# Attention before two gated layers: the value products of two chunks of keys and two heads made as one run of four

## The chip, the cores and the metric

The kernel runs on one core of one Trainium2 chip. The metric is the time of one execution on the device in microseconds (us); the median of several executions is compared. The engines are TensorE (PE, its weight loads PEld), VectorE (DVE), ScalarE (ACT), GpSimd (POOL) and SyncE (SP, which here issues transfers).

## The reference, cut to what matters

Attention over 4 batches of 12 heads with 448 tokens of 64 numbers, then a gated layer on all 1792 tokens, then a layer of 8 experts of which each token takes one:

```python
scores = scale * np.matmul(q_n, k_n.transpose(0, 1, 3, 2))   # q, k after RMS norm
scores = scores - np.max(scores, axis=-1, keepdims=True)
attn = np.exp(scores)
attn = attn / (np.sum(attn, axis=-1, keepdims=True) + 1e-09)
attn_out = np.matmul(attn, v)
...
x = moe(attn_out)      # (sigmoid(x @ w_gate) * (x @ w_val)) @ w_out
return moe2(x)         # one expert of two matrices for each token, chosen by a router
```

## The kernel before

Two heads of one batch are worked on together, 24 such head pairs, one after another. The 448 keys are cut into four chunks of 112 (CP, NCH). For each head pair there are eight score steps r = 0 to 7: chunk r // 2 of head r % 2. A score step (scores, L391 and L392) makes a 112 x 448 tile of keys against queries in PSUM out of two matmuls; the score tiles have two buffers (tag S). ScalarE turns it into exponentials (L394) in a tile of SBUF (tag PT, six buffers). The exponentials aren't normalised yet; for the divisor most of them are added up on GpSimd (L402), and over_sums adds over the keys with a matmul against ones, 64 columns for each head (rb, L434). There each head has one to three addends, by the stage (ADDS); the early head pairs have two of them, and so four matmuls.

The value product is weigh (L417). For a chunk of keys it takes, for each of the two heads, the chunk's 112 x 64 values as stationary and its 112 x 448 exponentials as moving operand, in fp32. Head 0 writes partitions 0 to 63 of the accumulator av, head 1 partitions 64 to 127, so the two matmuls use two halves of the array's columns. The accumulator has one buffer and gathers four chunks; then ScalarE copies it out (L427). The trace shows each fp32 matmul as two records.

Other work on TensorE around it: the row maxima are made ahead of the scores, one head pair earlier (maxima, m, L368), queries and keys are transposed (pq L309, pk L350), and the negated maxima too (pm L375).

attention is a generator of ticks. In each tick it gives up to two maxima, one score, at odd r one value product, and preparations of the next head pair. LAG and WLAG say how many ticks the scores follow the maxima and the value products the scores. The caller takes a step of the gated layer (glu, with its matmuls recorded at L680) between ticks when a batch is ready, and feeds weights. The final order on each engine is set by a scheduler that moves instructions by its own estimates. The helper beside ties matmuls together: each one after the first is given high priority and follows the one ahead of it.

Of the kernel before, what the change touches and what calls it, by code (L numbers as in the profile page):

```python
# [20 lines left out]
B, H, S, D = 4, 12, 448, 64  # L21
CP = 112
NCH = S // CP
# [82 lines left out]
def tile_kernel(ctx, tc, q, k, v, g_q, g_k, w_gate, w_val, w_out, emb, tau, w1, w2, out):  # L106
    nc = tc.nc
# [9 lines left out]
    def psum(tag, bufs, name):  # L117
        return ps.tile([P, 512], F32, tag=tag, name=name, bufs=bufs)
# [98 lines left out]
    def part_of(j):  # L217
        return slice(j * D, (j + 1) * D)
# [4 lines left out]
    def load(g):  # L223

        b, hp = divmod(g, H // 2)
        heads = slice(2 * hp, 2 * hp + 2)
        qk = [a1.tile([CP, 2, NCH, D], F32, tag="qk", name=f"{n}{g}", bufs=NQK) for n in ("qr", "kr")]

        def tokens(t, z=heads):
            return t[b, z].rearrange("h (p c) d -> p h c d", c=NCH)  # L230

        if g == 0:
            for i, t, j in ((0, q, 0), (1, k, 0), (0, q, 1), (1, k, 1)):
                (nc.scalar if i == 0 and j == 1 else nc.sync).dma_start(qk[i][:, j], t[b, 2 * hp + j].rearrange("(p c) d -> p c d", c=NCH))
            gains()
        else:
            nc.sync.dma_start(qk[0], tokens(q))
            nc.sync.dma_start(qk[1], tokens(k))

        def values():  # L240
            v_ = a2.tile([CP, 2, NCH, D], F32, tag="v", name=f"v{g}", bufs=2)
            nc.sync.dma_start(v_, tokens(v))
            return v_

        return qk, values
# [59 lines left out]
    def q_side(g, qn):  # L305

        pq = psum("T", 3, f"pq{g}")
        for c in range(NCH):
            nc.tensor.transpose(pq[:, c * CP:(c + 1) * CP], qn[:, c].rearrange("p h d -> p (h d)"), ident[:CP, :CP])  # L309
        X = []  # L310
        for j in range(2):
            xs = a2.tile([P, S], F32R, tag="X", name=f"X{g}_{j}", bufs=NX)
            a, z = part_of(j), part_of(1 - j)
            nc.scalar.activation(xs[a], pq[a, :S], AF.Copy, scale=gcol[a])  # L314
            nc.vector.scalar_tensor_tensor(out=xs[z], in0=pq[a, :S], scalar=gcol[a], in1=fv(xs[a]),
                                           op0=ALU.mult, op1=ALU.subtract)
            X.append(xs)
        return X
# [8 lines left out]
    def constants():  # L327

        one64 = state["one64"] = a2.tile([CP, D], F32, name="one64", bufs=1)
        nc.gpsimd.memset(one64, 1.0)  # L330
        identr = state["identr"] = a2.tile([CP, CP], F32R, name="identr", bufs=1)
        nc.gpsimd.tensor_copy(identr, ident[:CP, :CP])

        state["nm"] = [a2.tile([CP, NG + D], F32R, name=f"nm{i}", bufs=1) for i in range(2)]
        for t in state["nm"]:
            nc.gpsimd.tensor_copy(t, mhalf[:CP, 0:1].broadcast_to((CP, NG + D)))
        for i in range(4):
            t = a2.tile([P, S], F32R, tag=f"X2{i}", name=f"X2{i}", bufs=1)
            (nc.scalar.copy if i % 2 else nc.vector.tensor_copy)(t[upper], ident[upper, 0:1].broadcast_to((D, S)))
            shifted.append(t)  # L340
        for i in range(NY2):
            t = a2.tile([P, S], F32R, tag=f"Y2{i}", name=f"Y2{i}", bufs=1)
            (nc.scalar.copy if i % 2 else nc.vector.tensor_copy)(t[upper], ident[upper, D + i % 2:D + i % 2 + 1].broadcast_to((D, S)))
            picks.append(t)
# [35 lines left out]
    def again(g, st):  # L380

        for j in range(2):
            copy_on(DUP[stage(g)][j], shifted[(2 * g + j) % 4][lower], fv(st["X"][j][part_of(j)]))
# [20 lines left out]
    def beside(first, *others):  # L404

        got = first()
        with tc.high_priority():
            for fn in others:
                with tc.issue_after(got.ins):
                    got = fn()  # L410

    def weigh(g, kc, st):

        if kc == 0:
            st["av"] = psum("av", 1, f"av{g}")

        beside(*(lambda j=j: nc.tensor.matmul(st["av"][part_of(j), :S], lhsT=st["v"][:, j, kc], rhs=st["PT"][j, kc],  # L417
                                              start=kc == 0, stop=kc == NCH - 1) for j in (1, 0)))
        if kc == NCH - 1:
            b, hp = divmod(g, H // 2)  # L420
            if b < B - 1:
                xf[b, hp] = gp.tile([P, S], F32, tag="xf", name=f"xf{g}", bufs=6)
            else:
                if hp % 3 == 0:
                    xf["last"] = wp.tile([P, 3, S], F32, tag="r64", name=f"xf{g}", bufs=2)
                xf[b, hp] = xf["last"][:, hp % 3]
            nc.scalar.copy(xf[b, hp], st["av"][:, :S])  # L427
# [21 lines left out]
    def attention():  # L449

        np_ = B * H // 2
        raw = {0: load(0)}
        pair = {0: prepare(0, *raw[0])}
        raw[1] = load(1)
        constants()
        Y, X, st = {}, {}, {}
        X[0] = q_side(0, pair[0][0])
        Y[0] = k_side(0, pair[0][1])
        for t in range(NTICK):
            g, u = divmod(t, NG)  # L460
            if g < np_:
                if u == 0:
                    st[g] = dict(X=X.pop(g), Y=Y.pop(g), PT={}, sum={}, more=([], []),
                                 nm=state["nm"][g % 2])
                for i in range(MB):
                    if u % MB == 0:
                        maxima(g, u + i, st[g])
                if u == VAT:
                    st[g]["v"] = pair[g][2]()
                if u == AGAIN:  # L470
                    again(g, st[g])
                if u == NG - 1:
                    shifts(g, st[g])
            yield
            w, r = divmod(t - NG - LAG, NG)
            if 0 <= w < np_:
                scores(w, r, st[w])
            yield
            w, r = divmod(t - NG - LAG - WLAG, NG)
            if 0 <= w < np_ and r % 2:  # L480
                weigh(w, r // 2, st[w])
            for w in range(max(g - 3, 0), min(g + 1, np_)):
                if t == (w + 2) * NG - 1 + LAG + RLAG[stage(w)]:
                    over_sums(w, st[w])
            if g + 1 < np_ and u == PAT:
                pair[g + 1] = prepare(g + 1, *raw.pop(g + 1))
                if g + 2 < np_:
                    raw[g + 2] = load(g + 2)
            if g + 1 < np_ and u == XAT:
                X[g + 1] = q_side(g + 1, pair[g + 1][0])  # L490
            if g + 1 < np_ and u == YAT:
                Y[g + 1] = k_side(g + 1, pair[g + 1][1])
            yield
# [1087 lines left out]
```

## Time and profile before

| | |
|---|---|
| median of 3 runs | 1213.91 us (1213.56 to 1214.43) |
| profiled execution | 1212.88 us, of which its span is 1211.1 us |
| busy TensorE | 1149.8 us (95%) |
| busy weight loads | 939.8 us (78%) |
| busy DVE | 841.4 us (69%) |
| busy ACT | 665.1 us (55%) |
| busy POOL | 557.6 us (46%) |
| granted TensorE clock, mean | 0.987 of 2.4 GHz |

Shares are of the whole span. Attention runs from the start to about 621 us, mixed with the gated layer of the first batches from about 110 us on; the rest of the gated layer and the experts follow. The records of matmuls overlap in time, since a matmul's end is later than the next one's start; what one holds TensorE for is read from start to start.

### The profile page before, as it was taken

Reading aid. Unit: us, or ns where it says so; the run is one execution under the profiler, and the core shown is the slowest. Engines: PE = TensorE matmul, PEld = TensorE weight load, DVE = VectorE, ACT = ScalarE, POOL = GpSimd, SP = SyncE. Lnnn points to the kernel's source line nnn. Section 1 sums busy time; section 2 is a strip of 40 time slices with the busy share of each in tenths; the row PEclk is TensorE's granted clock in tenths of the full one; section 3 lists DMA queues with packets and bytes.
Section 4 is the critical chain, followed back from the end, with each engine's and each line's share of the span. In section 5 each row is a group of like instructions: output and inputs, shape, how many; then the busy total and the mean of one; then the engine's idle time right before and its main releaser. Section 6 shows DMA issues by size and latency. Waiting matters only on the chain. (4 is left out here: it accounts for less than half of the span.)

```text
span 1211.1 us, 18407 instructions
## 1 busy us (share of the span) xinstructions
PE 1149.8 (95%) x6516; PEld 939.8 (78%) x6517; DVE 841.4 (69%) x1415; ACT 665.1 (55%) x1239; POOL 557.6 (46%) x452
## 2 busy tenths in 40 slices
PE   3998899899999999999989999999998999999996
PEld 2444687677777777774578989998997999999996
DVE  6897889789768766766789983297456566555552
ACT  5888677777666555556644332243213555555652
POOL 4887976679667555657654430043314110011001
PEclk9999999899999999999999999999999999999998
DMA  4212666776632222210132222021256575777763
GB/s 120 57 51 86 211 217 215 225 223 214 202 113 88 92 93 88 83 42 23 56 89 66 66 66 66 27 65 53 80 150 188 160 213 164 231 232 217 219 203 101
DMA packets 151106, 156.15 MB, mean 129 GB/s; under 512 B 6947, under 2 KB 135205, under 8 KB 151010
## 3 DMA queue, kind: packets, MB, share of 16 engines
q1 hardware_dynamic: 148034, 143.07, 39.0%
q0 software_dynamic: 2848, 11.74, 2.8%
q8 instruction: 53, 0.87, 0.3%
q14 instruction: 43, 0.35, 0.1%
q10 hardware_dynamic: 128, 0.11, 0.0%
HBM read 129.74 MB, written 25.91 MB: 129 GB/s over the span
## 5 line engine op out<-in xcount | busy, mean ns | idle before, releaser
L585 DVE TENSOR_TENSOR wl<-wr,wh 128x768 fp32r<-128x768 f32 (+1 forms) x194 | 188.5, 972 | 142.1 <-ACT wh L582 123.5
L582 ACT CAST wh<-wr 128x768 fp32r<-128x768 f32 (+1 forms) x212 | 171.7, 810 | 178.8 <-DMA wr<-in_w_dram 50.6
L369 DVE TENSOR_REDUCE nm<-m 112x1 fp32r<-112x448 f32 x192 | 114.2, 615 | 33.2 <-PE m L368 31.3
L394 ACT ACTIVATE pt<-s 112x448 f32<-112x448 f32 x192 | 102.2, 542 | 63.0 <-PE s L392 57.9
L402 POOL TENSOR_TENSOR sum<-pt,sum 112x448 f32<-112x448 f32 x78 | 108.2, 1397 | 27.4 <-ACT pt L394 27.2
L271 POOL TENSOR_TENSOR ms<-ms,mhalf 112x8 f32<-112x8 f32 x46 | 85.6, 1860 | 36.6 <-ACT ms L270 36.4
L417 PE MATMUL av<-pt,v 112*64 112x448 f32 x384 | 97.1, 585 | 0.5 <-ACT pt L394 0.2
L402 POOL TENSOR_TENSOR sum<-pt,pt 112x448 f32<-112x448 f32 x48 | 60.9, 1273 | 62.0 <-ACT pt L394 54.1
L391 PEld LDWEIGHTS s<-X,Y 128*112 128x112 f32 x192 | 34.5, 180 | 68.0 <-issue 57.0
L391 PE MATMUL s<-X,Y 128*112 128x448 f32 x192 | 81.3, 424 | 5.6 <-ACT pt L394 5.4
L368 PE MATMUL m<-Y,X 128*112 128x448 f32 x192 | 71.7, 409 | 10.1 <-ACT X L314 5.8
L1289 POOL DMA_INDIRECT xe<-x2d,iu_all x16 | 18.6, 1162 | 123.4 <-PE pxe L1314 119.9
L392 PE MATMUL s<-X,Y 128*112 128x448 f32 x192 | 72.2, 382 | 3.2 <-ACT X L378 3.2
L368 PEld LDWEIGHTS m<-Y,X 128*112 128x112 f32 x192 | 34.1, 183 | 32.1 <-ACT Y L321 6.4
L1300 POOL DMA_INDIRECT out_dram<-orow,iu_all x16 | 17.2, 1077 | 89.1 <-ACT orow L1421 78.9
L623 DVE SCALAR_TENSOR_TENSOR wr<-r 128x768 int32<-128x768 int32 x36 | 41.1, 1141 | 24.6 <-ACT r L620 20.9
L625 DVE SCALAR_TENSOR_TENSOR wr<-r,wr 128x768 int32<-128x768 int32 x36 | 54.2, 1506 | 0.5
L680 PE MATMUL ph<-xeh,wh 128*128 128x256 f32 (+2 forms) x336 | 50.3, 284 | 0.0
L680 PE MATMUL ph<-xel,wh 128*128 128x256 f32 (+2 forms) x336 | 49.7, 282 | 0.0
L680 PE MATMUL ph<-xeh,wl 128*128 128x256 f32 (+2 forms) x336 | 49.4, 282 | 0.0
L585 POOL TENSOR_TENSOR wl<-wr,wh 128x768 fp32r<-128x768 f32 x18 | 37.0, 2056 | 20.7 <-ACT wh L582 20.7
L709 POOL TENSOR_TENSOR gl<-sg,gh 128x448 fp32r<-128x448 f32 x24 | 33.0, 1374 | 29.4 <-DVE gh L321 22.1
(778 smaller groups left out, 3050.3 us busy)
## 6 DMA issues: line engine op xcount, KB each, us to landing
wr<-in_w_dram SPq DMA_DIRECT2D x112, 384.0 KB, 3.9
wr<-w SPq DMA_DIRECT2D x72, 384.0 KB, 3.0
w<-wr SPq DMA_DIRECT2D x36, 384.0 KB, 2.8
r<-in_w_gate_dram SPq DMA_DIRECT2D x12, 768.0 KB, 5.0
r<-in_w_val_dram SPq DMA_DIRECT2D x12, 768.0 KB, 4.9
r<-in_w_out_dram SPq DMA_DIRECT2D x12, 768.0 KB, 4.6
wr<-in_w_dram SPq DMA_DIRECT2D x24, 256.0 KB, 2.9
v<-in_v_dram SPq DMA_DIRECT2D x24, 224.0 KB, 3.1
```

Source lines behind the costliest of these rows:

```text
L271: nc.gpsimd.tensor_tensor(m, m, mhalf[:CP, :m.shape[1]], ALU.pow)
L368: nc.tensor.matmul(s_[:CP, :S], lhsT=st["X"][j][:, c * CP:(c + 1) * CP], rhs=st["Y"][j][0], start=True, stop=True)
L369: last["max"] = nc.vector.tensor_reduce(st["nm"][:, 2 * c + j:2 * c + j + 1], s_[:CP, :S], axis=AX.X, op=ALU.max, negate=True)
L391: nc.tensor.matmul(s_[:CP, :S], lhsT=yh[:, z], rhs=st["X"][j], start=True, stop=False)
L392: nc.tensor.matmul(s_[:CP, :S], lhsT=yl[:, z], rhs=st["X2"][j], start=False, stop=True)
L394: last["exp"] = nc.scalar.activation(p_, s_[:CP, :S], AF.Exp)
L402: eng.tensor_tensor(st["sum"][j], p_, st["PT"][j, 0] if kc == 1 else st["sum"][j], ALU.add)
L417: beside(*(lambda j=j: nc.tensor.matmul(st["av"][part_of(j), :S], lhsT=st["v"][:, j, kc], rhs=st["PT"][j, kc], start=kc == 0, stop=kc == N ...
L582: nc.scalar.copy(hi, raw)
L585: eng.tensor_tensor(lo, raw, fv(hi), ALU.subtract)
L625: nc.vector.scalar_tensor_tensor(out=m, in0=high, scalar=-0x80000000, in1=m, op0=ALU.bitwise_and, op1=ALU.bitwise_or)
L680: nc.tensor.matmul(pt[:, :cols], lhsT=wts[i][a], rhs=xs[i][z], start=first and k == 1, stop=last and k == 3 * n)
```

## The change

weigh now takes a tuple of chunks instead of one. It is called at r = 3 and r = 7 with two chunks, where it was called at r = 1, 3, 5 and 7 with one. It issues four matmuls tied together: the newer chunk of head 1 and head 0, then the older chunk of head 1 and head 0. So the first of the four is the one that reads the newest exponentials. The flags start and stop sit on the first and the last chunk in that order. The code behind line 417 stands one line lower: L434 is L435 in the changed kernel, L680 is L681.

```diff
@@ -409,14 +409,15 @@
                 with tc.issue_after(got.ins):
                     got = fn()
-    def weigh(g, kc, st):
-
-        if kc == 0:
+    def weigh(g, kcs, st):
+
+        if 0 in kcs:
             st["av"] = psum("av", 1, f"av{g}")
-        beside(*(lambda j=j: nc.tensor.matmul(st["av"][part_of(j), :S], lhsT=st["v"][:, j, kc], rhs=st["PT"][j, kc],
-                                              start=kc == 0, stop=kc == NCH - 1) for j in (1, 0)))
-        if kc == NCH - 1:
+        beside(*(lambda j=j, kc=kc: nc.tensor.matmul(st["av"][part_of(j), :S], lhsT=st["v"][:, j, kc], rhs=st["PT"][j, kc],
+                                                     start=0 in kcs and kc == kcs[-1], stop=NCH - 1 in kcs and kc == kcs[0])
+                 for kc in reversed(kcs) for j in (1, 0)))
+        if NCH - 1 in kcs:
             b, hp = divmod(g, H // 2)
             if b < B - 1:
                 xf[b, hp] = gp.tile([P, S], F32, tag="xf", name=f"xf{g}", bufs=6)
@@ -477,8 +478,8 @@
                 scores(w, r, st[w])
             yield
             w, r = divmod(t - NG - LAG - WLAG, NG)
-            if 0 <= w < np_ and r % 2:
-                weigh(w, r // 2, st[w])
+            if 0 <= w < np_ and r % 4 == 3:
+                weigh(w, (r // 2 - 1, r // 2), st[w])
             for w in range(max(g - 3, 0), min(g + 1, np_)):
                 if t == (w + 2) * NG - 1 + LAG + RLAG[stage(w)]:
                     over_sums(w, st[w])
```

The order on TensorE, in the part of the program with attention alone (the second head pair's steps s_2 to s_7 and the maxima of the next). The tile names are s for scores with their r, av for the accumulator, pt for exponentials with their r. Before:

```order
L417 MATMUL av_460<-pt_3_466,v_294 64x448
L417 MATMUL av_460<-pt_2_456,v_294 64x448
L391 MATMUL s_5_516<-X_1_225,Y_249 112x448
L392 MATMUL s_5_516<-X_146,Y_154 112x448
L391 MATMUL s_6_528<-X_0_222,Y_245 112x448
L392 MATMUL s_6_528<-X_144,Y_152 112x448
L368 MATMUL m_7_485<-Y_360,X_1_311 112x448
L368 MATMUL m_0_522<-Y_501,X_0_441 112x448
L417 MATMUL av_460<-pt_5_519,v_294 64x448
L417 MATMUL av_460<-pt_4_491,v_294 64x448
L391 MATMUL s_7_552<-X_1_225,Y_249 112x448
L392 MATMUL s_7_552<-X_146,Y_154 112x448
```

A value pair stands ahead of s_5 and another one ahead of s_7.

TensorE in the changed kernel, the same place:

```order
L417 MATMUL av_491<-pt_3_463,v_294 64x448
L417 MATMUL av_491<-pt_2_456,v_294 64x448
L417 MATMUL av_491<-pt_1_434,v_294 64x448
L417 MATMUL av_491<-pt_0_419,v_294 64x448
L391 MATMUL s_5_516<-X_1_225,Y_249 112x448
L392 MATMUL s_5_516<-X_146,Y_154 112x448
L368 MATMUL m_7_482<-Y_360,X_1_311 112x448
L391 MATMUL s_6_528<-X_0_222,Y_245 112x448
L392 MATMUL s_6_528<-X_144,Y_152 112x448
L368 MATMUL m_0_522<-Y_501,X_0_441 112x448
L391 MATMUL s_7_550<-X_1_225,Y_249 112x448
L392 MATMUL s_7_550<-X_146,Y_154 112x448
```

The pair on pt_5 and pt_4 that stood between s_6 and s_7 is gone from there, and the pair on pt_1 and pt_0 has joined that on pt_3 and pt_2. Between the second matmul of s_5 and the first of s_7 there are four rows now; before there were four and the value pair.

TensorE near the end of attention, before, from s_6 of a late head pair (px is a matmul of the router):

```order
L391 MATMUL s_6_5839<-X_0_5312,Y_5402 112x448
L392 MATMUL s_6_5839<-X_140,Y_152 112x448
L368 MATMUL m_6_5775<-Y_5599,X_0_5509 112x448
L368 MATMUL m_7_5778<-Y_5603,X_1_5512 112x448
L417 MATMUL av_5730<-pt_5_5800,v_5495 64x448
L417 MATMUL av_5730<-pt_4_5784,v_5495 64x448
L391 MATMUL s_7_5853<-X_1_5315,Y_5406 112x448
L392 MATMUL s_7_5853<-X_142,Y_154 112x448
L391 MATMUL s_0_5859<-X_0_5509,Y_5599 112x448
L375 MATMUL pm_5789<-identr,nm_137 66x112 x4
L994 MATMUL px_0_0_5825<-beside_1250,x_0_5691 112x136 x2
```

One more px follows and then the pair on pt_7, so four rows stand between it and the second matmul of s_7.

TensorE in the changed kernel, the same place:

```order
L391 MATMUL s_6_5839<-X_0_5312,Y_5402 112x448
L392 MATMUL s_6_5839<-X_140,Y_152 112x448
L368 MATMUL m_7_5775<-Y_5603,X_1_5512 112x448
L391 MATMUL s_7_5851<-X_1_5315,Y_5406 112x448
L392 MATMUL s_7_5851<-X_142,Y_154 112x448
L391 MATMUL s_0_5857<-X_0_5509,Y_5599 112x448
L417 MATMUL av_5784<-pt_7_5854,v_5495 64x448
L417 MATMUL av_5784<-pt_6_5842,v_5495 64x448
L417 MATMUL av_5784<-pt_5_5800,v_5495 64x448
L417 MATMUL av_5784<-pt_4_5781,v_5495 64x448
```

Here the value pairs on pt_5 and pt_7 have become one run, and one row stands between the second matmul of s_7 and the run that reads pt_7.

In all, the 96 pairs of before stand as 48 unbroken runs of four. TensorE's last 3372 rows of 5699 are the same in both.

## Rows read from the trace of the kernel before

**Rows 1.** Windows: stretch, length, busy us (count) of PE, PEld, DVE, ACT, POOL, clock, DMA.
```profile
33.00:110.00 77.00, 74.81 (x350) 36.28 (x348) 68.38 (x114) 63.88 (x134) 65.67 (x51) 1.00 0.21 61
110.00:557.00 447.00, 432.18 (x2108) 322.65 (x2106) 341.20 (x481) 297.84 (x539) 299.44 (x214) 0.98 0.46 146
557.00:621.00 64.00, 61.18 (x283) 35.06 (x283) 49.02 (x77) 39.40 (x81) 44.36 (x37) 0.97 0.19 59
621.00:1211.00 590.00, 569.00 (x3743) 538.03 (x3741) 361.10 (x695) 245.68 (x448) 131.88 (x112) 0.99 0.45 134
```

**Rows 2.** Windows of line L417 alone: PE and PEld busy, clock, DMA.
```profile
33.00:110.00 77.00, 23.83 (x96) 4.84 (x96) 1.00 0.21 61
110.00:557.00 447.00, 56.04 (x222) 11.35 (x220) 0.98 0.46 146
557.00:621.00 64.00, 17.13 (x68) 3.55 (x68) 0.97 0.19 59
```

**Rows 3.** Timeline, TensorE: start us, length us, what; around one value pair.
```profile
48.40 0.36 PE L392 MATMUL s<-X,Y 128*112 128x448 f32 x1
48.60 0.37 PE L368 MATMUL m<-Y,X 128*112 128x448 f32 x1
48.90 0.97 PE L417 MATMUL av<-pt,v 112*64 112x448 f32 x4
49.80 0.46 PE L391 MATMUL s<-X,Y 128*112 128x448 f32 x1
50.10 0.36 PE L392 MATMUL s<-X,Y 128*112 128x448 f32 x1
```

**Rows 4.** Timeline, TensorE: the four sum matmuls of a head pair (L434).
```profile
44.57 0.55 PE L309 MATMUL pq<-ident,qn 112*128 112x112 f32 x4
45.05 0.97 PE L434 MATMUL rb<-pt,one 112*64 112x448 f32 x4
45.85 0.92 PE L434 MATMUL rb<-sum,one 112*64 112x448 f32 x4
46.70 0.46 PE L368 MATMUL m<-Y,X 128*112 128x448 f32 x1
47.00 0.36 PE L392 MATMUL s<-X,Y 128*112 128x448 f32 x1
```

**Rows 5.** Timeline, TensorE's weight loads inside that run.
```profile
45.48 0.14 PEld L434 LDWEIGHTS rb<-sum,one 112*64 112x64 f32 x2 [0.23 <-issue]
45.85 0.14 PEld L434 LDWEIGHTS rb<-sum,one 112*64 112x64 f32 x2 [0.23 <-issue]
```

**Rows 6.** TensorE's waits, 110 to 557 us: total us, times, longest.
```profile
PE pg L680 <- ACT sg L703: 3.6, 3, 2.3
PE s L391 <- ACT pt L394: 2.8, 2, 1.5
```

**Rows 7.** Timeline, TensorE: a value pair that waited (in brackets: idle, releaser).
```profile
42.89 0.97 PE L417 MATMUL av<-pt,v 112*64 112x448 f32 x4 [0.19 <-ACT pt L394]
```

**Rows 8.** Timeline, TensorE: a score that waited for an exponential.
```profile
572.07 0.46 PE L391 MATMUL s<-X,Y 128*112 128x448 f32 x1 [1.34 <-ACT pt L394]
```

**Rows 9.** Timeline, TensorE: scores on both sides of a value pair.
```profile
52.40 0.36 PE L392 MATMUL s<-X,Y 128*112 128x448 f32 x1
...
52.80 0.36 PE L392 MATMUL s<-X,Y 128*112 128x448 f32 x1
...
54.51 0.46 PE L391 MATMUL s<-X,Y 128*112 128x448 f32 x1
```

**Rows 10.** Timeline, ACT: the exponentials of the two scores of rows 9.
```profile
52.80 0.55 ACT L394 ACTIVATE pt<-s 112x448 f32<-112x448 f32 x1 [0.45 <-PE s L392]
...
53.92 0.54 ACT L394 ACTIVATE pt<-s 112x448 f32<-112x448 f32 x1
```

**Rows 11.** Windows: a stretch with waits, and the half-clock stretch behind it.
```profile
112.61:115.55 2.94, 1.83 (x8) 1.04 (x9) 1.04 (x2) 2.89 (x5) 1.73 (x2) 1.00 0.12 29
115.55:118.96 3.41, 3.41 (x11) 1.53 (x10) 2.47 (x4) 3.05 (x6) 1.57 (x1) 0.50 0.25 70
```

## The prediction, made before the changed kernel ran

> **What bounds the kernel now.** I read the share of each engine by stretch first, then TensorE's order of time around the edited line, then who made TensorE wait. The span falls into four stretches that matter [rows 1]: 33 to 110 us is attention alone, 110 to 557 us is attention with the matmuls of the gated layer (L680) filling TensorE between its steps, 557 to 621 us is the end of attention with little filler, and from 621 us on there is no value product left. TensorE (PE) is busy 74.81 of 77.00 us, 432.18 of 447.00, 61.18 of 64.00 and 569.00 of 590.00 [rows 1]. So it sets the pace in all four, and time that it no longer needs is time saved, as far as the next engine follows. Next in the first stretch are DVE at 68.38 us (89%), POOL at 65.67 and ACT at 63.88 of 77; in the second DVE has 76% and ACT 67% [rows 1]. The edited line shows 96 records in the first stretch, 222 in the second and 68 in the third [rows 2]. Each fp32 matmul is two records and a pair of heads is four, so these are 24, 55 and 17 pairs, 96 in all (two records straddle edges).
>
> **What the change removes.** A pair of value products uses 64 columns of the array per head. From its start at 48.90 to the next matmul at 49.80 it holds TensorE 0.90 us [rows 3]. It also makes its neighbours longer: the maximum's matmul ahead of it has 0.30 us before the pair starts (48.60 to 48.90), and the score matmul behind it has 0.30 (49.80 to 50.10), where the same kind of matmul inside a row of full-width ones has 0.20 (48.40 to 48.60) [rows 3]. That is 0.10 at each end, so a pair costs 0.90 + 0.20 = 1.10 us and two pairs 2.20.
>
> The trace of before has the very thing that the change makes: where both heads have two addends, the sums of a head pair stand as four matmuls of 64 columns in the same alternating order (rb, L434). That run goes from 45.05 to 46.70, or 1.65 us, with 0.30 for the matmul behind it (46.70 to 47.00) [rows 4]. The end ahead of it is hidden behind transposes there, so I take 0.10 for it too: 1.65 + 0.20 = 1.85. A merge saves 2.20 - 1.85 = 0.35 us by these rows; their last digit is 0.01, and I use 0.34. Of that 0.20 is one set of ends fewer, and 0.15 is that the run's second half follows without the first's tail (1.65 against 1.80). The order of the changed kernel has all 48 runs as four neighbouring rows, so 48 x 0.34 = **16.3 us**: 55 / 2 x 0.34 = 9.4 in the stretch with filler, 41 / 2 x 0.34 = 6.9 (7.0 by the rounded sum) in the two without. The number of matmuls, exponentials, additions and transfers is the same, and beyond 621 us TensorE's last 3372 of 5699 rows stand in the same order, so nothing is counted there but the earlier start.
>
> One rule speaks against it. The run's weight loads last 0.14 us and begin 0.37 us apart, 45.48 and 45.85, while the matmuls before them stream, and the run's second half takes 0.85 [rows 4, 5]: they cost nothing. The Trainium skill, TensorE: Matmul & The Clock Gate, Part 3, says that LDWEIGHTS overlaps with matmuls in flight "only when row_grp differs"; here every load goes to the same rows. By that rule two more loads in a row would lie open in each run; this case's row says they don't, and the row decides.
>
> **What it moves.** (a) *Where filler stands.* Here 17 or more rows lie between the newest score and the run, save at two places (9 and 4), so the run itself waits for nothing. Freed time can still be lost to ACT and DVE, on which TensorE waits there for 3.6 us (sigmoid), 2.8 us (exponentials) [rows 6] and less. Bounds: nothing lost, or all 9.4. Both engines have a quarter or more of this stretch free, so I take a tenth: 0.9 us.
>
> (b) *The exponential ahead of the run.* The run's first matmul reads the newest exponential, and all of TensorE's queue is behind it. With three rows between the score and the run's start before, TensorE waited 0.19 us [rows 7]; each row fewer adds one matmul's 0.20 [rows 3]. In the order there were six places with three rows; now there are four with three, two with two, one with one. At 0.19, 0.39 and 0.59 that is 0.76 + 0.78 + 0.59 = 2.1 against 1.1: 1.0 us more. Bounds: 0 (ACT late before as well) and 1.34 for each of the seven [rows 8], 9.
>
> (c) *The scores crowd together.* This is the main cost. The score tiles have two PSUM buffers, so a score must wait until the exponential two scores back is done. Before, a value pair lay between: the second matmul of s_5 at 52.40 and the first of s_7 at 54.51 are 2.1 us apart [rows 9]. Now a stretch of four scores has none between them. Its gap is four rows of 0.20 and the matmul itself, some 1.0 us. ACT needs 0.40 to start and 0.55 for the exponential when it is free (52.40 to 52.80, end 53.35), and more when a copy is ahead of it: the score at 52.80 (s_6) got its exponential at 53.92, 1.12 later, with the end at 54.46 [rows 9, 10]. So the gap is just enough for a free ACT and too short for a busy one. In the order I count 26 places in the stretches without filler where three or four rows, and no value or sum run, lie between; before, two, of three and of two rows (and four of a single row, where a score's second half was put off; now there is one). What each costs isn't in the trace: from nothing to 1.34 us, TensorE's longest wait for an exponential in these two stretches [rows 8], 0 to 35 us in all. A cost below nothing isn't excluded for one place, since a wait like that of 572 us may vanish in another order, but it is for the sum, as no engine but TensorE gets less to do. I take the row nearest in kind, 0.19 [rows 7], since ACT has 13 us of the first 77 free and catches up during the 1.65 us run: 26 x 0.19 = 4.9 us.
>
> (d) *At nothing:* value tiles and exponentials are held longer. There are six exponential tiles, and a run frees four of them one score after its newest; the exponential after the next is the first that needs one back. If that were late, ACT and then TensorE would wait as in (c). The accumulator is held from the first run to its copy, shorter than before. Transfers keep their count and their queues.
>
> Sum: 16.3 - 0.9 - 1.0 - 4.9 = 9.5 us. The profiled execution took 1212.88 us (its span 1211.1 and 1.8 around it), so 1203.4; the median of the runs is 1.03 above it: **1204.4 us**.
>
> **The rivals.** *All of it is kept* (chance 0.12): the scheduler puts maxima and transposes so that no exponential is late. The full 16.3 gives 1197.6. A half-clock stretch that follows a wait (2.94 us with TensorE busy 1.83, then 3.41 at 0.50, which is 1.2 instead of 2.4 GHz [rows 11]) may vanish too, worth half its length, 1.7: 1196. Against it: 89% of DVE becomes 94% in the first stretch (77 - 12 x 0.34 = 72.9).
>
> *Exponentials take what the runs gave* (0.12): the 26 places at 0.45 each are 11.7, and the sum 2.7: 1211.2, between 1209 and 1216 with its spread. For it: the score at 52.80 was served late in a stretch in which ACT still had pauses.
>
> *Slower* (0.10): the same places, but ACT's backlog doesn't drain in one run. It decides from 14.4 / 26 = 0.55 us each; at 0.8 the places cost 20.8 and the time is 1213.9 + 6.4 = 1220. Waits as long as that also precede half-clock stretches [rows 8, 11], each 1.7 more. Against it: the 1.65 us run leaves ACT three exponentials' time (0.55 each), and over the first stretch ACT has 13.1 us without work [rows 1].
>
> *Weight loads lie open in a run* (0.02): two loads of 0.14 in each run [rows 5] leave 0.06 of 0.34, 2.9 us in all, less 6.8: 1217.8. This is what the skill's rule above would give; the rb rows speak against it.
>
> *The run isn't run as one* (0.01): the chip serves the second pair as a new run; the 1.65 us row excludes it. 1213.9 or more.
>
> **How the numbers follow.** The forecast has 0.63 and, with places at 0 to 0.37 us, 1199 to 1209. The range for 8 in 10 runs from 1197 (about half of the first rival lies under it) to 1213 (the slower cases lie over it). A difference within 0.2%, 1211.5 to 1216.3, is about what a measurement of this kernel can't tell from no change. Faster: 0.63 + 0.12 + half of the second rival, 0.06, is 0.81. Same: 0.06 + 0.01 + 0.03 of the slower one's near end, 0.10. Slower: 0.07 + 0.02, 0.09.
>
> **What would show it.** Each run of four holds TensorE 1.65 us with 0.30 at its ends: if 1.85 or more, the first step is wrong. TensorE's waits of a score for an exponential grow from some 5 us to about 10, nearly all ahead of 110 us and after 557: if they stay, the first rival holds, if they pass 19, the slower one. The line's 97 us of busy time [rows 2] falls to about 48 x 1.65 plus tails, 83. The stretch with filler ends some 8 us nearer to the attention start, and 621 us comes at about 611. Unforeseen would be a change after attention, or many half-clock stretches more.

## The result, and the profile after

The changed kernel takes 1220.15 us in the median of six executions, the kernel before 1213.74 in the median of six: a ratio of 1.0052, with an interval of 1.0037 to 1.0067. It is slower by about 6.4 us. The forecast was 1204.4, with a range that ended at 1213.

The first lines of the page of the changed kernel: the span, and TensorE's busy time with its share.

```profile
span 1217.1 us, 18407 instructions
PE 1141.6 (94%) x6516; PEld 951.4 (78%) x6517; DVE 841.8 (69%) x1415; ACT 663.5 (55%) x1239; POOL 555.0 (46%) x452
```

Before, TensorE was busy 1149.8 of 1211.1 us. So it is busy 8.2 us less, and idle 75.5 instead of 61.3 us: 14.2 us more. The mean granted clock fell from 0.987 to 0.983 of 2.4 GHz in the two profiled executions; over the six executions of the changed kernel it is 0.982. The clock falls to 0.50 (1.2 GHz) in stretches of 3.41 us or twice that. In those of before TensorE is busy 23.87 us, in those after 33.77 (the sums of their windows; one more at the end of each program has no matmul in it). Half of that is what half clock cost: 11.9 us before and 16.9 after, 5 us more. At full clock the busy time would have fallen by some 13 us. That is the account of the whole result: 13 us of work saved, 14 us of idle time and 5 us of clock added. Spans and clocks of the two:

```profile
core 0: 1217.1 us, clock 0.983
```
```profile
core 0: 1211.1 us, clock 0.987
```

The sums of the windows at half clock, before and after:

```profile
sum 23.87, PE 23.87 PEld 12.36 DVE 16.82 ACT 16.21 POOL 15.91; mean PE 3.98 PEld 2.06 DVE 2.80 ACT 2.70 POOL 2.65
```
```profile
sum 37.54, PE 33.77 PEld 25.90 DVE 24.70 ACT 20.97 POOL 17.43; mean PE 4.22 PEld 3.24 DVE 3.09 ACT 2.62 POOL 2.18
```

The run itself does what the row of the sums had promised. The changed kernel's timeline of TensorE around one run (start us, length us, what; x8 are the eight records of four matmuls):

```profile
51.81 0.36 PE L392 MATMUL s<-X,Y 128*112 128x448 f32 x1
52.10 1.72 PE L417 MATMUL av<-pt,v 112*64 112x448 f32 x8
53.75 0.46 PE L391 MATMUL s<-X,Y 128*112 128x448 f32 x1
54.05 0.36 PE L392 MATMUL s<-X,Y 128*112 128x448 f32 x1
```

From 52.10 to 53.75 it holds TensorE 1.65 us, with 0.29 ahead and 0.30 behind: as in [rows 4], against 0.90 for a pair in [rows 3]. Outside half clock 42 of 46 runs hold it 1.65 or 1.66 us, and 88 of 92 pairs before 0.90. The idle time is elsewhere. TensorE's longest waits over the span that differ, in the kernel before (total us, times, longest):

```profile
PE s L391 <- ACT pt L394: 5.4, 5, 1.5
...
PE pm L375 <- DVE nm L369: 2.8, 2, 1.6
PE m L368 <- ACT Y L321: 2.4, 4, 0.8
...
PE m L368 <- DVE Y L358: 0.8, 1, 0.8
...
PE av L417 <- ACT pt L394: 0.2, 1, 0.2
```

and in the changed kernel:

```profile
PE m L368 <- DVE Y L358: 6.6, 2, 5.8
PE m L368 <- ACT Y L321: 5.7, 9, 1.8
PE s L391 <- ACT pt L394: 5.0, 9, 1.3
PE pm L375 <- DVE nm L369: 4.8, 4, 1.7
...
PE m L368 <- DVE nm L369: 2.8, 3, 2.0
PE av L417 <- ACT pt L394: 2.7, 4, 1.2
PE rb L435 <- DVE nm L369: 1.9, 2, 1.7
```

The scores' waits for exponentials are the same in sum (5.4 and 5.0 us), though there are nine now, all of them ahead of 120 us, where the kernel before had 1.9 us of them. What grew are the maxima's waits, for the keys that ScalarE and DVE make (2.4 to 5.7 and 0.8 to 6.6) and for the buffers that DVE's reductions free (0 to 2.8), their transposes (2.8 to 4.8) and sums (0 to 1.9) behind such reductions, and the value run's own wait (0.2 to 2.7).

How a stretch without filler looks now, TensorE's timeline of the changed kernel (in brackets: idle time and its releaser):

```profile
36.87 0.46 PE L391 MATMUL s<-X,Y 128*112 128x448 f32 x1
37.17 0.36 PE L392 MATMUL s<-X,Y 128*112 128x448 f32 x1
37.37 0.36 PE L391 MATMUL s<-X,Y 128*112 128x448 f32 x1
37.56 0.37 PE L392 MATMUL s<-X,Y 128*112 128x448 f32 x1
37.77 0.57 PE L368 MATMUL m<-Y,X 128*112 128x448 f32 x2
39.18 0.46 PE L391 MATMUL s<-X,Y 128*112 128x448 f32 x1 [0.84 <-ACT pt L394]
39.48 0.37 PE L392 MATMUL s<-X,Y 128*112 128x448 f32 x1
39.68 0.36 PE L368 MATMUL m<-Y,X 128*112 128x448 f32 x1
40.30 0.46 PE L391 MATMUL s<-X,Y 128*112 128x448 f32 x1 [0.26 <-ACT pt L394]
40.60 0.37 PE L368 MATMUL m<-Y,X 128*112 128x448 f32 x1
41.77 1.02 PE L417 MATMUL av<-pt,v 112*64 112x448 f32 x2 [0.81 <-ACT pt L394]
```

Two scores start 0.50 us apart, the third waits, the fourth waits, and the run waits for an exponential. The next row is the window of 3.41 us that starts within the last of these waits, at a granted clock of 0.50. In it this run takes from 41.77 to 44.96, 3.19 us instead of 1.65:

```profile
41.58:44.99 3.41, 3.22 (x9) 0.80 (x9) 0.05 (x1) 0.59 (x2) 1.95 (x2) 0.50 0.23 67
```

By stretch, the windows of the changed kernel (stretch, length, busy us and count of PE, PEld, DVE, ACT, POOL, clock, DMA share, GB/s), as [rows 1] are for before:

```profile
33.00:114.00 81.00, 71.88 (x338) 35.94 (x338) 65.09 (x111) 62.25 (x133) 62.21 (x50) 0.98 0.17 51
114.00:563.00 449.00, 425.43 (x2109) 330.44 (x2105) 343.15 (x479) 294.96 (x534) 293.53 (x212) 0.98 0.46 146
563.00:622.00 59.00, 55.06 (x272) 33.27 (x274) 46.34 (x76) 41.17 (x86) 46.65 (x38) 1.00 0.19 57
622.00:1217.00 595.00, 575.46 (x3761) 542.86 (x3757) 364.63 (x700) 246.56 (x449) 135.14 (x113) 0.98 0.45 133
```

In the first stretch TensorE falls from 97% busy to 89%. The start of the first score of a head pair is a mark of progress that both kernels have. At that of the second head pair the changed kernel is 1.4 us ahead (40.30 against 41.70), at the seventh 3.8 behind (111.05 against 107.21), at the ninth 13.3 behind (189.75 against 176.47, with some filler moved ahead of it), and at the last score of attention 1.3 behind (616.1 against 614.8). Behind that last score stand 18 records more than before, 14 of filler and one pair of value products, some 3.6 us at 0.20 each (an estimate), so at equal work it is some 5 us behind there. The idle time that the change added is early: 5.2 us between the first scores of the second and the seventh head pair (windows further below), 5.5 from there to the ninth (the one wait of 5.8 us, shown below, lies there), 2.9 to the thirteenth, 2.1 to the last score. From the last score on there is 1.5 us less of it, but those 3.6 us of work, and two stretches at half clock that last 6.83 us each where they lasted 3.41: 2.7 of the 5 us of clock. So the loss of idle time is early, and the span behind attention, where the prediction had called any change unforeseen, is 4.7 us longer. From the seventh head pair to the ninth, and from the last score on, before and then after:

```profile
107.21:176.47 69.26, 63.15 (x291) 44.23 (x289) 55.17 (x73) 52.74 (x92) 52.91 (x45) 0.95 0.60 192
614.84:1211.10 596.26, 575.16 (x3772) 542.81 (x3770) 365.75 (x701) 247.05 (x450) 133.74 (x113) 0.99 0.44 133
```
```profile
111.05:189.75 78.70, 67.06 (x313) 50.39 (x313) 62.46 (x80) 58.91 (x103) 55.59 (x46) 0.93 0.61 194
616.10:1217.10 601.00, 581.36 (x3789) 547.69 (x3787) 368.74 (x706) 248.81 (x454) 138.81 (x116) 0.98 0.45 133
```

### The profile page after: what moved, and what is told of

Its sections match the earlier page's. It is cut to its first block, busy times and chain, and to the rows that moved or that the text cites. A ratio compares the mean times of both kernels' runs of the same rounds, so it can differ in the third digit from the quotient of the medians.

```text
span 1217.1 us, 18407 instructions
## 1 busy us (share of the span) xinstructions
PE 1141.6 (94%) x6516; PEld 951.4 (78%) x6517; DVE 841.8 (69%) x1415; ACT 663.5 (55%) x1239; POOL 555.0 (46%) x452
## 5 line engine op out<-in xcount | busy, mean ns | idle before, releaser
L586 DVE TENSOR_TENSOR wl<-wr,wh 128x768 fp32r<-128x768 f32 (+1 forms) x194 | 191.3, 987 | 146.2 <-ACT wh L583 118.2
L402 POOL TENSOR_TENSOR sum<-pt,sum 112x448 f32<-112x448 f32 x78 | 103.5, 1334 | 14.5 <-ACT pt L394 12.6
L271 POOL TENSOR_TENSOR ms<-ms,mhalf 112x8 f32<-112x8 f32 x46 | 82.4, 1791 | 41.7 <-ACT ms L270 41.5
L417 PE MATMUL av<-pt,v 112*64 112x448 f32 x384 | 84.2, 560 | 2.8 <-ACT pt L394 2.7
L368 PEld LDWEIGHTS m<-Y,X 128*112 128x112 f32 x192 | 34.3, 185 | 41.2 <-ACT Y L321 10.9
L624 DVE SCALAR_TENSOR_TENSOR wr<-r 128x768 int32<-128x768 int32 x36 | 46.8, 1300 | 20.2 <-ACT r L621 13.4
L586 POOL TENSOR_TENSOR wl<-wr,wh 128x768 fp32r<-128x768 f32 x18 | 40.2, 2232 | 36.7 <-ACT wh L583 33.4
L417 PEld LDWEIGHTS av<-pt,v 112*64 112x64 f32 x384 | 23.8, 138 | 40.2 <-issue 27.3
L681 PE MATMUL ph<-xeh,wh 128*128 128x256 f32 (+2 forms) x336 | 50.2, 284 | 0.0
L681 PE MATMUL ph<-xel,wh 128*128 128x256 f32 (+2 forms) x336 | 49.7, 282 | 0.0
L681 PE MATMUL ph<-xeh,wl 128*128 128x256 f32 (+2 forms) x336 | 49.4, 282 | 0.0
```

The costliest lines, as they stand in the source:

```text
L271: nc.gpsimd.tensor_tensor(m, m, mhalf[:CP, :m.shape[1]], ALU.pow)
L368: nc.tensor.matmul(s_[:CP, :S], lhsT=st["X"][j][:, c * CP:(c + 1) * CP], rhs=st["Y"][j][0], start=True, stop=True)
L402: eng.tensor_tensor(st["sum"][j], p_, st["PT"][j, 0] if kc == 1 else st["sum"][j], ALU.add)
L417: beside(*(lambda j=j, kc=kc: nc.tensor.matmul(st["av"][part_of(j), :S], lhsT=st["v"][:, j, kc], rhs=st["PT"][j, kc], start=0 in kcs and k ...
L586: eng.tensor_tensor(lo, raw, fv(hi), ALU.subtract)
L681: nc.tensor.matmul(pt[:, :cols], lhsT=wts[i][a], rhs=xs[i][z], start=first and k == 1, stop=last and k == 3 * n)
```

## The experiments

Each run was compared with runs of the kernel before on the same chip at the same time, whose median was 1212.7 to 1214.1. "Run" is a kernel with runs of four, "pair" its control with pairs. Their medians are good to some 2 to 5 us, by the intervals of their ratios, so a smaller difference between two kernels isn't shown by the medians alone.

### Where the loss sits: runs of four in a part of the head pairs

Theory A was that scores crowd where no filler stands; theory B, the rival, that the scheduler's other order costs by chance. Two kernels with the change in one part each:

```diff
-            if 0 <= w < np_ and r % 4 == 3:
+            if 0 <= w < np_ and r % 4 == 3 and w < 8:
                 weigh(w, (r // 2 - 1, r // 2), st[w])
+            elif 0 <= w < np_ and r % 2 and not w < 8:
+                weigh(w, (r // 2,), st[w])
```

Early (w < 8), expected:

> Runs of four only for head pairs 0 to 7 (16 of the 48 runs), pairs as before from head pair 8 on. Theory A (a run crowds four scores together; where no filler stands, ScalarE cannot serve the exponentials in time, so TensorE waits for them and for what ScalarE and DVE make late): the loss sits here. The trace of the changed kernel is 13 us behind at the first score of head pair 8, some 3 of it moved filler; so 1213.7 + 5 to 10 = 1219 to 1224, with TensorE's waits for exponentials ahead of 110 us at 4 us or more. Theory B (the scheduler's other order and the half-clock stretches behind chance waits cost it, not the crowding): no tie to this stretch, 1213.7 less 16 x 0.34 = 5.4, give or take 4: 1204 to 1213.

Late (w >= 8 in both places), expected:

> Pairs for head pairs 0 to 7, runs of four from head pair 8 on (32 of 48 runs). Theory A: 32 x 0.34 = 10.9 us less, with 3 to 4 us of it lost at the end of attention and in the filler: 1205 to 1208, faster than before. Theory B: the loss is spread with the reordering, so this gains no more than a third of the runs would, and may lose: 1210 to 1220.

The early one takes 1218.79 us, ratio 1.0046 (1.0023 to 1.0070), at the lower end of theory A's range and far over theory B's; the late one 1209.32, ratio 0.9967 (0.9949 to 0.9986). The same edit loses in the first eight head pairs and gains in the others. The early kernel's time from the first score of the second head pair to that of the seventh is 70.8 us, the changed kernel's own; the late one has 65.5, as before. The late one gains 3.4 us, a third of the 10.9 us that its 32 merges save: less than theory A expected, and as much as theory B allowed. The early one's scores wait 3.2 us for exponentials ahead of 110 us, where theory A asked for 4 or more.

The profiled executions, counted as above, say why. TensorE's busy time at full clock falls by 6.3 us in the early kernel and by 11.3 in the late one, so all of the saving arrives (5.4 and 10.9). Early, 5.8 us of idle time and 3.6 us of half clock are added to it; late, 1.4 us of idle time and 6.6 us of half clock. So what sits in the first eight head pairs is the idle time, and the clock costs in both. The two results don't add up to the change's (6.1 - 3.4 = 2.7 against 6.4), which is within their intervals.

### How much is the chance of one order

```diff
-SETUP = 185
+SETUP = 188
```

With runs, expected:

> The changed kernel with the router's setup placed three ticks later (188 instead of 185), nothing else. The changed kernel has a wait of 5.8 us of TensorE at 146 us, behind a DVE instruction of 4.8 us in the router setup's stretch. Theory A: that wait is chance and may go or stay, the rest of the loss stays: 1215 to 1221. Theory B: most of the loss is such chance, so with another order the time falls to 1213 or less, or rises to 1225.

With pairs, expected:

> The kernel before with the router's setup three ticks later: the size of chance. Theory A: within 3 us of 1213. Theory B: moves by more than 3 us either way, as small changes of order do.

The longest new wait of the changed kernel stands in the router setup's stretch. A maximum on TensorE waits 5.78 us there for keys that DVE makes. Its row, and that of DVE ahead of it:

```profile
146.12 0.71 PE L368 MATMUL m<-Y,X 128*112 128x448 f32 x1 [5.78 <-DVE Y L358]
```
```profile
138.87 4.79 DVE L624 SCALAR_TENSOR_TENSOR wr<-r 128x768 int32<-128x768 int32 x1 [1.86 <-DMA x2d<-zr]
```

DVE waited for a transfer, took 4.79 us for a weight's words, made two more steps on weights, and only then came to the keys. With the setup three ticks later this wait isn't there. Still the run takes 1220.34 us and the pair 1213.87: 6.5 us apart, as the change alone (6.4). So that wait was chance, and the loss didn't hang on it; other waits took its place. Two other orders are few, and 6.5 is good to some 3 us: the executions of this run kernel spread from 1211 to 1225 us, and they do so with the clock. Three with a mean granted clock of 0.987 or 0.988 took 1211.5 to 1214.1, as its pair; seven with 0.978 to 0.983 took 1219.3 to 1225.1.

### Do ScalarE and DVE lack time?

Theory A was split here into three. A1: ScalarE lacks time for the crowded exponentials. C: DVE lacks it for its keys and maxima. A2: scores and maxima come in bursts on few PSUM buffers, and lose time even where the engines have some to spare. Three pairs of kernels relieve them in head pairs 2 to 7. ScalarE's copies left out:

```diff
-                if u == AGAIN:
+                if u == AGAIN and not 2 <= g < 8:
```

With runs, expected:

> The changed kernel without part of the computation: for head pairs 2 to 7 the two ScalarE copies of 0.55 us that refresh the lower half of the second query operand (again) are left out, 1.1 us of some 10.9 us of ScalarE per head pair. Theory A (ScalarE, crowded by four scores in a row, is what TensorE waits for in the stretch without filler): with ScalarE relieved, this against the pairs with the same left out is at most 2 us slower, or faster by up to 5, where the change alone is 6.4 slower; waits for exponentials ahead of 110 us fall from 4.2 to under 2.5 us. Theory B (chance of the scheduler's order): the difference stays at 3 to 9 us.

With pairs, expected:

> The kernel before with the same copies left out for head pairs 2 to 7: the control of the run above. TensorE sets the pace here with pairs, so both theories expect little: 1208 to 1214.

DVE's maxima over half the keys:

```diff
-nc.vector.tensor_reduce(..., s_[:CP, :S], axis=AX.X, op=ALU.max, negate=True)
+nc.vector.tensor_reduce(..., s_[:CP, :S // 2 if 2 <= g < 8 else S], axis=AX.X, op=ALU.max, negate=True)
```

With runs, expected:

> The changed kernel; for head pairs 2 to 7 the eight row maxima are taken over the first 224 of the 448 keys (the shift cancels in the division), which takes about 0.25 us off each of eight DVE reductions of 0.615, some 2 us of DVE's 11.9 per head pair. In the changed kernel TensorE's waits grew most where a maximum waits for what DVE and ScalarE make (0.8 to 6.6 us and 2.4 to 5.7). Theory C (DVE, at 89%, sets the pace of the early stretch as soon as TensorE's value products shrink): this against its control is no slower, down to 6 us faster. Theory A2 (bursts on two score buffers): it stays 3 to 7 us slower.

With pairs, expected:

> The kernel before with the same shorter maxima: the control. TensorE sets the pace with pairs, so 1209 to 1214 by theory A2 and by C; well under 1209 would say that DVE held the pairs up too.

Both edits together, with runs, expected:

> The changed kernel with the shorter maxima and, for head pairs 2 to 7, without the two ScalarE copies of the second query operand (left out, as in the earlier pair): DVE has 2 us and ScalarE 1.1 us of a head pair's 12.6 more to spare. Theory C and A1 (engines lack time): against its control 3 to 6 us faster, the whole saving of the runs. Theory A2: still 2 us or more slower.

With pairs, expected:

> The kernel before with the same shorter maxima and left-out copies: the control. 1207 to 1214.

| relieved | run, us | pair, us | run less pair | the early stretch: run, pair, us |
|---|---|---|---|---|
| nothing | 1220.15 | 1213.74 | +6.4 | 70.8, 65.5 |
| ScalarE | 1218.37 | 1214.98 | +3.4 | 66.6, 62.5 |
| DVE | 1233.25 | 1216.68 | +16.6 | 76.2, 67.4 |
| both | 1218.94 | 1214.66 | +4.3 | 71.8, 67.9 |

The early stretch is from the first score of the second head pair to that of the seventh. With DVE relieved, the windows of this stretch, of the run, have DVE busy 47.55 of 76.22 us, 62%, and TensorE no faster:

```profile
42.86:119.08 76.22, 67.48 (x300) 32.36 (x301) 47.55 (x97) 54.47 (x115) 53.76 (x44) 0.93 0.16 46
```

In no case is the run faster than its pair, which a lack of time on these engines would have asked for. The 3.4 with ScalarE relieved is less than 6.4 by no more than the noise, and the scores of that run wait 3.5 us for exponentials ahead of 110 us, where the changed kernel's list has 3.2 (the expectation had 4.2 falling under 2.5). The three pairs lie 0.7 to 2.7 us above the ranges expected of them. Half clock distorts the early stretch: it cost 1.7 us in the run with nothing relieved, 5.1 with DVE and 1.7 with both relieved, and 3.4 in the pair with both. Without it the run is 3.5, 4.1, 3.7 and 5.6 us behind its pair, in the order of the table: relief doesn't shrink that.

That the run with DVE relieved is 13 us slower than the change alone is not explained: less work on an engine gave another order, with five microseconds of this stretch lost to the clock (0.93 of 76.22). If the order is all of it, it shows how much an order can cost here.

### Do two score buffers hold it up?

```diff
-s_ = psum("S", 2, f"s{g}_{r}")
+s_ = psum("mm" if g < H // 2 and r % 4 > 1 else "S", 2, f"s{g}_{r}")
-s_ = psum("mm" if g < H // 2 else "T", 2 if g < H // 2 else 3, f"m{g}_{u}")
+s_ = psum("T", 3, f"m{g}_{u}")
```

Four buffers in head pairs 0 to 5, with runs, expected:

> The changed kernel, and for head pairs 0 to 5 the scores have four PSUM buffers instead of two (the second two from the buffers that the early maxima had; those use the three shared ones). Theory A: a score no longer waits for the exponential two back, so the waits of scores for exponentials ahead of 110 us fall from 4.2 us to under 1.5, and this against the pairs with the same buffers is faster by 5 us or more. Theory B: this against the pairs with the same buffers is about what the change is, 3 to 9 us slower.

With pairs, expected:

> The kernel before with the same four score buffers for head pairs 0 to 5: the control of the run above. Both theories: within 5 us of 1213.7, since its scores waited 1.5 us for exponentials in this stretch, and maxima may wait for the shared buffers.

A third buffer from the shared ones, the maxima's left alone:

```diff
-s_ = psum("S", 2, f"s{g}_{r}")
+s_ = psum(*(("T", 3) if g < H // 2 and r % 3 == 2 else ("S", 2)), f"s{g}_{r}")
```

With runs, expected:

> The changed kernel; for head pairs 0 to 5 every third score takes one of the three shared PSUM buffers, so the scores have three buffers and the maxima keep theirs. What the earlier runs left: theory A1, ScalarE lacks time (weakened: relieving it by 10% sped up pairs and runs alike), and theory A2, two score buffers can't cover the way from a score to its exponential and back once four scores stand in a row. By A2 this against the pairs with the same three buffers is no slower, 0 to 5 us faster, and waits of scores for exponentials ahead of 110 us fall under 2 us. By A1 and by B it stays 3 to 8 us slower than its control.

With pairs, expected:

> The kernel before with the same three score buffers for head pairs 0 to 5: the control. Pairs waited 1.5 us for exponentials there, so A2: 1211 to 1216; the shared buffers may be short for the transposes, which would add to this and to the run above alike.

With four buffers the run takes 1225.98 us and the pair 1236.80, with three the run 1218.02 and the pair 1231.47. So runs are now faster than pairs, by 10.8 and 13.4 us, as theories A and A2 asked by their letter. But both controls were expected near 1213, and are 18 to 24 us over it, by which these two comparisons lose their worth. That the shared buffers were short, and pairs suffered from that more, is a reading; no run here shows it. The run with three is 2 us faster than the changed kernel, which is within the noise. With four buffers the scores still wait 2.2 us ahead of 110 us (under 1.5 had been expected). TensorE's waits in the run with three, from 33 to 115 us:

```profile
PE m L368 <- DVE nm L369: 4.0, 5, 1.2
PE m L368 <- ACT Y L321: 2.3, 2, 1.9
```

No score waits for an exponential in this list any more, where the changed kernel has 2.5 us of such waits from 33 to 110 us. The maxima wait instead. So the two buffers make the scores' waits, but taking them away moves the waits rather than ending them.

### Is TensorE's idle time slack?

```diff
-        nc.tensor.matmul(s_[:CP, :S], lhsT=st["X"][j][:, c * CP:(c + 1) * CP], ...)
+        for _ in range(2 if 2 <= g < 8 else 1):
+            nc.tensor.matmul(s_[:CP, :S], lhsT=st["X"][j][:, c * CP:(c + 1) * CP], ...)
```

This gives TensorE work, and no other engine. With runs, expected:

> The changed kernel; for head pairs 2 to 7 each of the 48 maxima's matmuls is made twice into the same tile, 48 x 0.205 = 9.8 us of TensorE work more, and nothing more on any other engine. If TensorE's waits in the early stretch of the changed kernel are slack (the run took work away that had covered the way of scores and maxima through the other engines: theory A2), added work fills the waits and costs little: at most 5 us more than the changed kernel's 1220, so under 1225. If what is late there is tied to TensorE's own order (theory B: another chance order, with TensorE still setting the pace), the full 9.8 us are added: 1230.

With pairs, expected:

> The kernel before with the same doubled maxima: the control, in which TensorE is busy 97% of the stretch, so it pays the 9.8 us: 1221 to 1225. By theory A2 run minus pair falls from 6.4 us to about zero or below; by theory B it stays near 6.4.

The run takes 1224.74 us and the pair 1223.45. Beside the 1220.15 and 1213.74 of the same kernels without the added work, these are 4.6 and 9.7 us more, for 9.8 us of matmuls, each good to some 4 us. By the medians pairs pay all of it and runs half, and run and pair are 1.3 us apart instead of 6.4. The early stretch's windows, of before, of the changed kernel, and of the pair and the run with doubled maxima:

```profile
41.70:107.21 65.51, 63.80 (x307) 30.46 (x305) 58.66 (x99) 54.98 (x117) 55.32 (x43) 1.00 0.19 54
```
```profile
40.30:111.05 70.75, 63.88 (x300) 31.40 (x300) 55.61 (x96) 53.96 (x115) 52.85 (x44) 0.98 0.17 50
```
```profile
41.41:113.11 71.70, 69.92 (x347) 37.41 (x345) 59.71 (x99) 55.88 (x117) 54.90 (x44) 1.00 0.16 49
```
```profile
40.40:114.84 74.44, 70.72 (x344) 39.20 (x345) 59.26 (x97) 53.83 (x115) 52.55 (x44) 0.98 0.16 47
```

TensorE is idle for 1.71 us of this stretch before and 6.87 after (length less busy), and with the added work 1.78 and 3.72. DVE's share falls from 89.5% to 78.6% by the change. So in the changed kernel no engine is full there: each waits for another for part of the time. Forty of the 48 added matmuls, 8.2 us, lie in this stretch, and 3.2 us of the run's idle time there are gone. The stretch grew by 3.7 us for the run and by 6.2 for the pair. This is as theory A2 expected.

It isn't the whole of the 1224.74 us, however. Over the span of the profiled executions, the run's idle time falls only from 75.5 to 73.9 us, and its busy time at full clock rises by 10.9 us. What gives back 4.0 us is the clock: TensorE is busy 25.7 us at half clock instead of 33.8. (The pair has 2.2 us more of idle time, 8.4 of busy time at full clock and 1.1 of half clock.) So that the added work filled slack is shown for the early stretch, in part; that it explains the time isn't.

### Runs of four where they gain

The edit of the first two experiments, with w >= 12 and with w >= 20. From head pair 12 on, expected:

> Runs of four only from head pair 12 on (24 of 48 runs). With runs from head pair 8 on the trace gained nothing in head pairs 8 to 11 (153.8 against 151.7 us) and 8 us from there to the end of attention. Theory A (early loss, late gain): 24 x 0.34 = 8.2 less 2 to 4 for waits and clock, 1207 to 1210, at least as fast as from head pair 8. Theory B: anywhere between 1207 and 1216.

In the last four, expected:

> Runs of four only for the last four head pairs (8 of 48 runs), where little filler stands but ScalarE is busy 62% instead of 83%. Theory A1 (loaded engines make the loss): 8 x 0.34 = 2.7 gained, 1209 to 1212. Theory A2 (four scores in a row with two buffers lose wherever no filler stands): no gain, 1213 to 1215.

From head pair 12 on it takes 1206.11 us (ratio 0.9936, 0.9913 to 0.9959), 6.9 us less than the kernel before and the best of all; 8.2 had been the whole saving of its 24 merges. Its profile has 8.4 us less of busy time at full clock, 3.4 us more of idle time and 0.4 us less of half clock. In the last four head pairs alone it takes 1209.11 (0.9969, 0.9953 to 0.9985): a gain of 3.9 where 2.7 was the saving, which lies within the interval (1.8 to 5.7). These last head pairs have little filler too, and they gain, against theory A2; it isn't the missing filler alone that makes the loss. What differs is how loaded the other engines are there, DVE 77% and ACT 62% against 89% and 83% early [rows 1]. But the kernels with both engines relieved above have DVE at 67% and ScalarE at 69% in the early stretch, and still lose. And the program itself treats head pairs differently by number: from head pair 6 on the maxima use other PSUM buffers, and at 6 and at 12 the sums and copies are shared out another way among the engines. Which of these makes the difference wasn't tried.

## Why the prediction failed, step by step

The profiled execution is 6.0 us longer by its span, where the sum had it 9.5 shorter: 15.5 us apart. Of these, up to rounding, 7.4 are idle time (14.2 us came, where the sum's (a), (b) and (c) had allowed 6.8), 5.0 are half clock, which had no term, and 3.2 are saving that didn't show (13.1 of 16.3).

*TensorE sets the pace* held for the kernel before, as far as the doubled maxima show it: pairs pay 9.7 us for 9.8. *The run saves 0.34 us for each merge* held: 1.65 us, ends of 0.30. The value products' line falls from 97.0 us to 84.2, where 83 was said. Of the 16.3 us of the whole change 13.1 show as busy time at full clock; the kernels with runs in a part of the head pairs show all of theirs (6.3, 11.3 and 8.4 us for 5.4, 10.9 and 8.2). Where the other 3 us went stays open. *The rule of the Trainium skill on open weight loads* (TensorE: Matmul & The Clock Gate, Part 3) was rightly overruled by [rows 5]: the run of 1.65 us is as long as the sums' own, and has no room for a load in the open.

*(a) A tenth lost beside filler* fits, within the noise, from head pair 12 on, where 6.9 of 8.2 us arrived. It was too little from head pair 8 to 11: there the late kernel gains nothing, 156.8 us from the first score of head pair 8 to that of 12, against 156.9 before.

*(b) The run's wait for its newest exponential* was to grow by 1.0 us and grew by 2.5 (0.2 to 2.7). It was the right wait and somewhat too small.

*(c) The crowded scores* is the step that failed. The prediction saw that the value pairs between the scores had covered their way through ScalarE, and priced that at 26 places of 0.19 us, 4.9 in all, on scores that wait for exponentials. These waits do appear early (1.9 to 5.0 us ahead of 120 us), but over the span they grew nothing (5.4 to 5.0), since the later ones went. Apart from the tenth in (a), the waits of everything else behind the value products were put at nothing. By the two lists above those of the maxima grew by 3.3, 5.8 and 2.8 us, those of the transposes and sums by 2.0 and 1.9: 15.8 us in all, of which 5.8 are the one wait at 146 us; some other waits fell. That engines had time to spare didn't prevent it: relief of ScalarE and DVE left the loss. The reading here is that the head pairs are a loop through four engines, and that TensorE, by handing on two value products in one block, hands on everything else later or in bursts; no run shows the loop itself.

*The clock* had no term in the sum, only 1.7 us in a rival, and cost 5.0 us. Every half-clock stretch with matmuls in it, before and after, begins within a wait of TensorE or up to two microseconds behind one. Within attention five of them are new, at 41.6, 144, 256.6, 314.6 and 372.7 us, for instance that within the wait of 5.8 us, and three of before are gone (136.0, 231.6 and 572.9): 2.2 us more in sum. The other 2.7 us are the two longer ones behind attention, where the matmuls are the same; why they lasted longer isn't shown.

*The rival "slower"* had the time, 1220, and its direction, but by luck. Its price was laid on scores that wait for exponentials, which were to pass 19 us and stayed at 5.0. By the prediction's own sign ("if they stay, the first rival holds") all of the saving should then have been kept. The crowding was right, and the wait that shows it wasn't.

What stays open: which part of the loop holds the early stretch up. Relief of ScalarE and DVE didn't turn the loss, so it isn't their throughput alone; a third buffer took the scores' waits away, and the maxima wait instead. Whether another hand-written order of scores and maxima would keep the gain there wasn't tried. And of the changes of order that the scheduler made, the runs show the size, a few microseconds to more than ten, and not the reasons.

## What to carry to other kernels

A busy engine's work between two steps of another engine's chain can be cover. Before merging such pieces into a block, list everything that arrived in time behind them, not only the consumer of the next step. A saving on the busiest engine isn't yet a saving of time: here 13 us of it arrived, and 14 us of idle time and 5 us of half clock were added. Count what half clock costs as a term of its own, from the stretches at a granted clock of 0.50 and TensorE's busy time in them; it also moves between executions of one kernel, so compare several. An edit that is good for the engine itself should be tried by part of the program: here the same edit loses 0.5% in the first eight head pairs and gains 0.6% in the last twelve.

## What the runs showed of the hardware

Four fp32 matmuls of 64 columns, two on each half of the array, take 1.65 us in a row where two pairs of them take 0.90 each; the neighbours at either end have 0.30 us instead of 0.20, so the switch from and to full-width matmuls costs 0.10 at each end. At a granted clock of 0.50 such a run took 3.19 us. Less work on an engine made two kernels slower, in another order by the scheduler: with maxima of half the length the pair takes 1216.68 us (ratio 1.0031, 1.0018 to 1.0045) and the run 1233.25.
